# Products of zeros put in where TensorE's plan shows a wait, in the first units of a fused attention and token-mixing kernel

## The chip, the cores and the metric

The kernel runs on one core of one Trainium2 chip. The metric is device time in microseconds (us) of one execution; the number given for a kernel is the median of its runs. TensorE (PE in the profile) does the matrix products, VectorE (DVE), ScalarE (ACT) and GpSimd (POOL) the elementwise work, and SyncE's queue (SP) issues the transfers. Instructions of one engine run in the order in which they stand in the program.

## The reference

One block of a conditioned transformer, batch 1, 2048 tokens of width 512, all in bf16. The conditioning vector gives six vectors of width 512; then a windowed attention (32 heads of 16, each token sees itself and the 255 before it) and an MLP that mixes over tokens, each in a gated residual:

```python
mod = (_silu(c) @ w_mod).reshape(c.shape[0], 6, 1, -1)
sa, ca, ga, sb, cb, gb = (mod[:, n] for n in range(6))
h = _layernorm(x, axis=-1) * (1 + ca) + sa
x = x + ga * _A_ref(h, A_wqkv, A_wo)                   # sliding-window attention
h = _layernorm(x, axis=-1) * (1 + cb) + sb
x = x + gb * _B_ref(h, B_w1, B_b1, B_w2, B_b2)         # layernorm, then gelu(h over tokens @ w1 + b1) @ w2 + b2
```

## The kernel before

The 2048 tokens are 16 blocks of 128 and four groups of 512. The kernel has a hand-written start, a planned middle and a hand-written end.

**The start** (`warm`, `fm`, `turn`, lines 551 to 650) brings in the first tokens and weights, issues some 128x512 products of the tile `zero` with itself into a bank that nobody reads (`warm`, line 571; `WARM = (7, 1, 2)`), makes the modulation vectors, and turns, modulates and projects the first 256 tokens.

**The planned middle.** From there to about 165 us of the trace a planner decides, while the program is being built, in which order every engine's instructions stand. It keeps a clock of its own for each engine (`pe["t"]` for TensorE, `free[...]` for the others) in planned microseconds, asks for the earliest next step of each engine, emits the step that starts first, and moves that engine's clock on. TensorE's steps are of these kinds:

- a score step (`do_scores`, products on line 696): for a unit of a head group, the scores of four heads of 16, out of `QT` and `KT`, with the window's triangles added by products with `mask_w` and `mask_r`. It goes into one or two of three double banks of PSUM, named `t`. ACT takes the exponential of each (line 704, one `ACTIVATE` of 128x1024 or 128x768), and the bank is free after that;
- an attention step (`do_av`, line 721): exponentials times values for one head group, also into a `t` bank; DVE turns it (line 734) and divides;
- one product at a time of a dense group (`do_dense`) into one of two single banks named `dn`: the projections for queries and keys (line 356), which DVE or ACT copy out (lines 287, 369, 367), for values `V` (line 331, copied out on line 287), the turning of the normalized tokens of the first group (line 309, modulated on line 297), the broadcast modulation vectors (line 402), the output projection (line 432), and early parts of the MLP (line 470).

`pick_pe` picks between these; the main loop then calls the step with its planned start, `best[0]`. Where that is later than `pe["t"]`, TensorE waits by the plan. `issue` also books when TensorE's own instructions have to be fetched (`FIRST_BLOCK`, `BLOCK`, `FETCH`).

The tokens of the second group of 512 are normalized on DVE and POOL (`xn`, line 256), turned by four transfers of SP's queue (`turn_block`, line 305) into `h1T`, and modulated in place on DVE (line 297). SP's queue issues, in its fixed order: the weights, `wmod` (line 221), the biases, seven of the eight pieces of `wod` (line 224), the four turns, the last piece of `wod`, eight blocks of `x` (line 227), the broadcast vectors (line 418), the spread of keys `ks` into `KT` (line 385), the turns of the third group.

**The end** sums the first MLP product over all tokens (lines 462, 1334), applies gelu, and does the second product (line 1475) into the output.

A pool hands out a bank as a new tile each time; whoever writes the new tile first waits until the last use of the old one is over. If the old tile's last use was a write of TensorE itself that nobody read, the new writer waits for that write to be complete.

Of the kernel before, what the change touches and what calls it, by code (L numbers as in the profile page):

```python
# [8 lines left out]
DT = mybir.dt  # L9
# [3 lines left out]
P = 128  # L13
# [41 lines left out]
EARLY = 11  # L55
AHEAD = 14
PAUSE = 1.2
TURN_LAT = 2.5
FETCH, FIRST_BLOCK, BLOCK = 3.4, 193, 256
ODD = 0.31  # L60
# [3 lines left out]
def kernel(  # L64
# [14 lines left out]
    nc = tc.nc  # L79
# [62 lines left out]
    zero = modw.tile([P, 4 * P], DT.bfloat16, name="zero")  # L142
# [159 lines left out]
    def turn_block(tg, tl):  # L302
        if h1T[tg] is None:
            h1T[tg] = hpool.tile([P, ND, 4 * P], DT.bfloat16, name="h1T")
        dma.dma_start(out=h1T[tg][:, :, tl * P : (tl + 1) * P], in_=xn1[tg, tl][:], transpose=True)
# [219 lines left out]
    with tc.manual_schedule():  # L525

        dn_pools = [
            tc.alloc_tile_pool(name=f"ps_dn{n}", bufs=1, space=bass.MemoryType.PSUM, side="right") for n in range(2)
        ]
# [109 lines left out]
        t_pools = [tc.alloc_tile_pool(name=f"ps_t{n}", bufs=1, space=bass.MemoryType.PSUM) for n in range(3)]  # L639
# [154 lines left out]
        def publish(key, t):  # L794
            avail[key] = t
            for j in waiting.pop(key, []):
                j.settle()
# [96 lines left out]
        n = 2 * EARLY_HEADS  # L894
# [32 lines left out]
        def load_next(t):  # L927

            w1_state["busy"] = bool(loads)
            if not loads:  # L930
                return
            o, i = loads.pop(0)
            key = token()

            def then(t):
                loaded_at.append(t + 4.0)
                load_next(t + PAUSE)
            Job(lambda eng: eng.memset(o[:, 0:1], 0.0), {GE: 0.12}, gives=key, prio=4, at=t).settle()
            Job(lambda eng: dma.dma_start(out=o, in_=i), {YE: 0.6}, [key], prio=6, at=t, then=then).settle()
# [9 lines left out]
        def apply_jobs(tg, t, prio):  # L949
            used = [(k, tg - 2, g) for g in range(ND) for k in ("qd", "kd", "v") if tg > 1]  # L950
            for tl in range(4):
# [6 lines left out]
                    lambda eng, tl=tl: turn_block(tg, tl), {YE: 1.35}, [("x", tg, tl)] + used,  # L958
                    ("xt", tg, tl), 1, lat=TURN_LAT, at=t, then=lambda t, tl=tl: publish(("xe", tg, tl), t + 1.6),
                ).settle()  # L960
# [30 lines left out]
        pe = {"t": 0.0, "mode": "full", "group": (halves[2], 0), "s": 0, "av": 0, "n": 2 + 2 * (25 + 4 * ND + sum(WARM)), "block": -9.0}  # L991
        SWITCH = 0.094
        t_free, d_free = [0.0, 0.75, 0.0], [None, 0.0]
# [260 lines left out]
        def pick(e):  # L1254
            best = None
            able = [j for j in queue[e] if j.gate is None or j.gate()]
            if not able:
                return None
            first = min(begin(e, j) for j in able)
            if e == SE:  # L1260
                j = min((j for j in able if begin(e, j) <= first + 0.01), key=lambda j: (j.prio, j.seq))
            else:
                j = min((j for j in able if begin(e, j) <= first + VE_WIN), key=lambda j: (j.prio, j.seq))
            return begin(e, j), j

        def pick_pe():
            s, a, d, f = scores_start(), av_start(), dense_start(), first_start()
            if f and (a is None or f[0] < a[0] - 0.1) and (d is None or f[0] <= d[0] + 0.1):
                return f[0], do_first, f[1:]
            if a and (s is None or a[0] <= s[0] + AV_S) and (d is None or a[0] <= d[0] + AV_D):  # L1270
                return a[0], do_av, a[1:]
            if s and (d is None or s[0] <= d[0] + S_D):
                return s[0], do_scores, s[1:]
            if d:
                return d[0], do_dense, d[1:]
            return None

        while True:
            best = pick_pe()
            for e in (SE, VE, GE, YE):  # L1280
                c = pick(e)
                if c and (best is None or c[0] < best[0]):
                    best = c[0], e, c[1]
            if best is None:
                break
            if callable(best[1]):
                best[1](best[0], *best[2])
                continue
            start, e, j = best
            queue[e].remove(j)  # L1290
            j.emit(ENG[e])
            free[e] = start + j.opts[e]
            if e == VE and j.opts[e] == FAST:
                fast_until[0] = free[e]
            if j.then:
                j.then(free[e])
            if j.gives:
                publish(j.gives, free[e] + j.lat)
# [150 lines left out]
    with tc.tile_pool(name="ftmp", bufs=3) as ftmp, tc.tile_pool(  # L1449
        name="ps_y0", bufs=4, space=bass.MemoryType.PSUM  # L1450
    ) as ps_y0, tc.tile_pool(name="ps_y1", bufs=4, space=bass.MemoryType.PSUM) as ps_y1:
        for tg in range(NT // 4):
# [20 lines left out]
            for fc, (tl, lo, hi) in order:  # L1473
# [3 lines left out]
                    rhs=gated[fc][:] if last and (lo, hi) == LAST[-1] else guT[fc][:, lo:hi],  # L1477
                    start=(fc == 0), stop=(fc == NF - 1),
# [51 lines left out]
```

## Time and profile before

| what | us |
|---|---|
| median of 3 runs | 247.29 |
| the runs | 247.29, 250.26, 246.52 |
| the profiled execution, device time | 248.87 |
| its span, from the first to the last instruction | 246.7 |
| outside the span (248.87 - 246.7) | 2.17 |
| busy in the span: PE, DVE, ACT | 229.8, 190.0, 158.5 |

Times within the trace are counted from the start of the span. A row of the timeline gives the start, the length, the engine, the line, the operation with its tiles, shapes and the number of merged instructions; in square brackets stands the idle time of the engine before the row and what ended it, where there was a notable wait. In a row of stretches, `PEclk` is the share of its full clock that TensorE was granted.

### The profile page before, as it was taken

The page shows a single profiled execution, that of the slowest core. Times are in us where ns is not written, and L with a number is a line of the kernel's source. Part 1 is how long each engine was busy: PE and PEld are TensorE (multiplying, and loading weights), DVE is VectorE, ACT ScalarE, POOL GpSimd, SP SyncE. Part 2 cuts the span into 40 slices and gives each one's busy share as a digit, 9 for nine tenths or more (in the row PEclk, how much of TensorE's full clock was granted, in tenths as well). Part 3 has the DMA queues.
Part 4 walks back from the last instruction along what each step waited for, and adds up shares of the span by engine and source line. Part 5 has one row for each costly group of instructions (what it writes and reads, how often), then busy time and mean ns, then how long its engine had stood idle before and what let it go on. Part 6 is the DMA issues. An engine that isn't in the chain of part 4 may idle for free.

```text
span 246.7 us, 8687 instructions
## 1 busy us (share of the span) xinstructions
PE 229.8 (93%) x3691; PEld 122.6 (50%) x3723; DVE 190.0 (77%) x416; ACT 158.5 (64%) x182; POOL 69.7 (28%) x158
## 2 busy tenths in 40 slices
PE   5877999999999788999999999999999999999995
PEld 2544675655566365454454554544444444444444
DVE  5697679998999999999997989957974632543564
ACT  3495897999999898999999999950108700000000
POOL 7636104332272332423413624403540000000000
PEclk9996899999999999999999999999999999999999
DMA  6994455287573611010013131059995000201031
GB/s 202 314 351 129 88 148 131 43 139 160 168 98 74 152 25 27 5 21 3 9 23 79 51 88 45 3 169 352 415 409 224 0 3 0 85 23 64 27 103 43
DMA packets 32042, 27.70 MB, mean 112 GB/s; under 512 B 16516, under 2 KB 27652, under 8 KB 32004
## 3 DMA queue, kind: packets, MB, share of 16 engines
q1 hardware_dynamic: 31708, 26.63, 38.3%
q8 instruction: 29, 0.48, 0.9%
q10 hardware_dynamic: 296, 0.53, 0.6%
q14 instruction: 9, 0.07, 0.1%
HBM read 22.03 MB, written 2.10 MB: 98 GB/s over the span
## 4 chain that ended last, share of the span: by engine, by line
PE 74%; DVE 12%; ACT 6%; DMA 3%; issue 3%; SPq 0%; DVEq 0%; ACTq 0%
PE py L1475 20%; PE t L696 12%; PE dn L470 9%; PE dn L356 7%; PE t L462 6%; ACT et L704 6%; PE t L721 5%; PE dn L331 4%; PE dn L432 4%; PE t L1334 3%; DVE KT L369 3%; DMA wmod<-in_w_mod_dram 2%; PE pu L1334 2%; DVE QT L287 1%; PE pa L1370 1%
## 5 line engine op out<-in xcount | busy, mean ns | idle before, releaser
L704 ACT ACTIVATE et<-t 128x1024 bf16<-128x1024 f32 (+1 forms) x142 | 131.8, 1021 | 8.0 <-PE t L696 7.3
L1475 PE MATMUL py<-guT,w2r 128*128 128x512 bf16 (+2 forms) x234 | 47.7, 363 | 0.2
L696 PE MATMUL t<-QT,KT 32*128 32x64 bf16 (+4 forms) x752 | 38.0, 253 | 1.4 <-ACT et L704 0.9
L356 PE MATMUL dn<-h1T,wqkv 128*128 128x512 bf16 (+1 forms) x140 | 33.6, 357 | 4.9 <-DVE QT L287 1.8
L1475 PEld LDWEIGHTS <-w2r 128*128 128x128 bf16 x252 | 23.5, 98 | 25.4 <-DVE gelu_a L1357 0.4
L748 POOL TENSOR_TENSOR merge<-t,zr 128x512 bf16<-128x512 f32 (+1 forms) x16 | 21.5, 1346 | 42.8 <-DVE zr L743 42.7
L1490 DVE SCALAR_TENSOR_TENSOR o<-py,bFM,bc_gb 128x512 bf16<-128x512 f32 (+2 forms) x17 | 12.1, 711 | 24.5 <-PE py L1475 23.0
L696 PEld LDWEIGHTS <-KT 32*128 32x128 bf16 x752 | 13.9, 93 | 27.0 <-issue 25.1
L696 PE MATMUL t<-mask_r,mask_w 32*128 32x128 bf16 (+3 forms) x432 | 24.8, 223 | 0.4 <-issue 0.4
L470 PE MATMUL dn<-hb,w1hi 128*128 128x512 bf16 x91 | 23.9, 381 | 0.9 <-issue 0.6
L734 DVE STREAM_TRANSPOSE t<-t 128x1024 f32<-128x1024 f32 x16 | 19.8, 1236 | 4.2 <-PE t L721 4.1
L356 PEld LDWEIGHTS <-wqkv 128*128 128x128 bf16 x160 | 14.2, 102 | 16.3 <-issue 4.5
L231 POOL TENSOR_SCALAR ln_ve<-ln_mv 128x1 f32<-128x1 f32 x32 | 7.7, 241 | 48.0 <-DVE ln_mv L831 39.4
L235 POOL TENSOR_TENSOR ln_rstd<-ln_ve,mhalf 128x1 f32<-128x1 f32 x32 | 19.2, 601 | 2.7
L721 PEld LDWEIGHTS <-V 64*32 64x32 bf16 x1504 | 16.5, 91 | 6.6 <-issue 6.3
L721 PE MATMUL t<-et,V 64*32 64x320 bf16 (+4 forms) x1384 | 19.3, 251 | 0.0
L331 PE MATMUL dn<-wqkv,h1T 128*64 128x256 bf16 x256 | 17.6, 276 | 1.4 <-DVE V L287 0.9
L696 PEld LDWEIGHTS <-mask_w 32*128 32x128 bf16 x432 | 14.1, 95 | 2.7 <-issue 0.6
L331 PEld LDWEIGHTS <-h1T 128*64 128x64 bf16 x256 | 12.9, 109 | 3.4 <-issue 2.4
L470 PEld LDWEIGHTS <-w1hi 128*128 128x128 bf16 x98 | 8.1, 97 | 10.5 <-issue 3.0
L432 PE MATMUL dn<-wod,OTd 128*128 128x512 bf16 x43 | 12.2, 381 | 0.7 <-issue 0.3
L287 DVE CAST V<-dn 128x512 bf16<-128x512 f32 x15 | 10.1, 676 | 2.1 <-PE dn L331 2.1
(123 smaller groups left out, 289.3 us busy)
## 6 DMA issues: line engine op xcount, KB each, us to landing
w2r<-in_B_w_dram SPq DMA_DIRECT2D x14, 512.0 KB, 10.2
w1hi<-in_B_w_dram SPq DMA_DIRECT2D x11, 320.0 KB, 4.0
w1b<-in_B_w_dram SPq DMA_DIRECT2D x5, 448.0 KB, 6.7
x<-in_A_x_dram SPq DMA_DIRECT2D x16, 128.0 KB, 3.6
wmod<-in_w_mod_dram SPq DMA_DIRECT2D x4, 512.0 KB, 9.3
out_dram<-otile SPq DMA_DIRECT2D x15, 128.0 KB, 1.7
wqkv<-in_B_w_dram SPq DMA_DIRECT2D x11, 128.0 KB, 2.8
wqkv<-in_A_wqkv_dram SPq DMA_DIRECT2D x4, 256.0 KB, 6.0
```

The source lines that it names most:

```text
L235: nc.gpsimd.tensor_tensor(out=r[:], in0=ve[:], in1=mhalf[:, 0:n], op=ALU.pow)
L331: nc.tensor.matmul(pv[CH * par : CH * par + CH, 256 * ch : 256 * ch + 256].rearrange("p (h d) -> p h d", d=DH), lhsT=h1T[tg][:, dc, t0 : t ...
L356: nc.tensor.matmul(pq[:, 0:n_cols], lhsT=wqkv[:, dc, col0 : col0 + P], rhs=h1T[tg][:, dc, cols], start=(dc == 0), stop=(dc == ND - 1),)
L432: nc.tensor.matmul(pa[:], lhsT=tokens_of(OTd[tg][g], tl), rhs=wod[:, g, :], start=(g == 0), stop=(g == ND - 1),)
L462: nc.tensor.matmul(first[k][1][:, n, :], lhsT=w1_of(sc, 2 * k + n), rhs=hb[sc][:], start=(sc == 0), stop=(sc == NT - 1),)
L470: nc.tensor.matmul(ps[:], lhsT=w1_of(s0 + n, fc), rhs=hb[s0 + n][:], start=(n == 0), stop=(s0 + n + 1 == s1),)
L696: nc.tensor.matmul(o, lhsT=w, rhs=r, start=start, stop=stop, tile_position=(row, 0), skip_group_check=True,)
L704: nc.scalar.activation(out=state["e", u][:, 2 * a : 2 * a + 2, 0:w], in_=ps[:, :, 0:w], func=ACT.Exp, scale=SCORE_SCALE,)
L721: nc.tensor.matmul(chunks(o, qs), lhsT=Vring[kc // GC % 3][rows, kc % GC, h : h + 32], rhs=e[:, at : at + len(qs), :], start=first, stop=F ...
L734: nc.vector.transpose(out=v["t"][:].rearrange("p a c -> p (a c)"), in_=po[:].rearrange("p a c -> p (a c)"))
L748: eng.tensor_tensor(out=v["m"][:].rearrange("p (b d h) -> p h b d", d=DH, h=4)[:, :, lo:hi], in0=view()[:, :, lo:hi, 0:DH], in1=v["z"][:, ...
L1475: nc.tensor.matmul(pys[tl, lo, hi][:, 0 : hi - lo], lhsT=w2r[:, fc, tb * P : (tb + 1) * P], rhs=gated[fc][:] if last and (lo, hi) == LAST[ ...
```

## The change

A function `keep_busy` is called before each step of TensorE with the planned start of that step. If the plan shows a wait of at least 0.35 planned us that ends before `BUSY_UNTIL` (24 planned us), and one of the three `t` banks or two `dn` banks is free by the plan within 0.1 us, it takes a tile of the first such pool and issues one product of `zero` with itself, 128x512, for each 0.25 us of the wait less 0.1. Nobody reads the result. The planner's clock and its count of TensorE's instructions stay as they were, so all later decisions are the same.

```diff
@@ -55,6 +55,7 @@
 PAUSE = 1.2
+BUSY_UNTIL = 24.0
 TURN_LAT = 2.5
@@ -1275,6 +1276,17 @@
+        def keep_busy(until):
+
+            n = int((until - pe["t"] - 0.1) / 0.25)
+            pools = [
+                pool for pool, x in [*zip(t_pools, t_free), *zip(dn_pools, d_free)] if x is not None and x < pe["t"] + 0.1
+            ]
+            if n > 0 and pools and until < BUSY_UNTIL and pe["t"] > 0:
+                ps = pools[0].tile([P, 4 * P], DT.float32, name="dn" if pools[0] in dn_pools else f"t{t_pools.index(pools[0])}")
+                for _ in range(n):
+                    nc.tensor.matmul(ps[:], lhsT=zero[:, 0:P], rhs=zero[:], start=True, stop=True)
+
         while True:
             best = pick_pe()
@@ -1284,6 +1296,7 @@
             if callable(best[1]):
+                keep_busy(best[0])
                 best[1](best[0], *best[2])
                 continue
```

In the program this adds nine products with nine weight loads, at seven places on TensorE (7466 rows instead of 7448), all into `t` banks. Nothing moves on DVE, ACT, POOL or SP. Counted in order, places 1 to 4 get one product each, place 5 two, place 6 one, place 7 two:

1. before the eight projections that follow the first scores;
2. before the second score step;
3. before the third score step;
4. before the fourth score step;
5. before the last two key and query projections ahead of the fifth score step;
6. among the projections after the next score steps, where a `dn` bank is waited for;
7. before the score step that follows the turning of the biases (line 422).

Place 2 on TensorE, before. `t0`, `t1` and `t2` are the three banks for scores, a new number is a new tile:

```order
L356 MATMUL dn_437<-h1T_310,wqkv_132 128x256
L696 LDWEIGHTS KT0_167
L696 MATMUL t1_449<-QT1_421,KT0_167 128x256
L696 LDWEIGHTS KT0_167
L696 MATMUL t0_450<-QT1_421,KT0_167 128x256 [waits Activation_49]
```

The same place now (all line numbers are 1 or more higher, since the change adds lines):

```order
L357 MATMUL dn_439<-h1T_310,wqkv_132 128x256
L1288 LDWEIGHTS zero_134
L1288 MATMUL t1_451<-zero_134 128x512 [waits PE_49]
L697 LDWEIGHTS KT0_167
L697 MATMUL t1_453<-QT1_421,KT0_167 128x256 [waits PE_49]
L697 LDWEIGHTS KT0_167
L697 MATMUL t0_454<-QT1_421,KT0_167 128x256 [waits Activation_49]
```

The product of zeros takes the bank `t1` that the scores are about to take, and the first score product now waits until it is complete (`waits PE_49`); the wait of the second bank for ACT stands where it stood. At places 3, 4 and 7 the first score product waits for the product of zeros in the same way, and the wait for ACT has moved from it to the product of zeros.

Place 5 on TensorE, before:

```order
L356 MATMUL dn_565<-h1T_310,wqkv_132 128x256
L356 LDWEIGHTS wqkv_132 [waits DVE_49]
L356 MATMUL dn_578<-h1T_310,wqkv_132 128x256 [waits PE_49]
L356 MATMUL dn_578<-h1T_310,wqkv_132 128x256
L696 LDWEIGHTS KT0_167 [waits DVE_49]
L696 MATMUL t1_583<-QT0_374,KT0_167 128x64 [waits Activation_49]
L696 MATMUL t0_584<-QT0_374,KT0_167 128x64 [waits Activation_49]
```

The same place now:

```order
L357 MATMUL dn_573<-h1T_310,wqkv_132 128x256
L1288 LDWEIGHTS zero_134
L1288 MATMUL t0_586<-zero_134 128x512 [waits Activation_49]
L1288 MATMUL t0_586<-zero_134 128x512
L357 LDWEIGHTS wqkv_132 [waits DVE_49]
L357 MATMUL dn_589<-h1T_310,wqkv_132 128x256 [waits PE_49]
L697 MATMUL t1_594<-QT0_374,KT0_167 128x64 [waits DVE_49]
L697 MATMUL t0_595<-QT0_374,KT0_167 128x64 [waits PE_49]
```

Two products of zeros stand ahead of the projection that waits for DVE, in the bank `t0`; they wait for ACT to have left that bank, and the score product that uses it next waits for them, a few products later.

## The prediction
> **What bounds the kernel now.** I read the page first: its span, and the line of TensorE's granted clock by fortieths (6.17 us each).
>
> ```profile
> span 246.7 us, 8687 instructions
> PE 229.8 (93%) x3691; PEld 122.6 (50%) x3723; DVE 190.0 (77%) x416; ACT 158.5 (64%) x182; POOL 69.7 (28%) x158
> PEclk9996899999999999999999999999999999999999
> ```
>
> PE is busy 93% of the span, so whatever delays PE early is hard to win back. Its clock is full except in the fourth and fifth slices. The second view cuts that place into stretches of 3.41 us, half of the slow time, with two later stretches for comparison:
>
> ```profile
> core 0: us, PE busy (x) PEld busy (x) DVE busy (x) ACT busy (x) POOL busy (x), PEclk, DMA share, GB/s
> 13.43:16.84 3.41, 2.80 (x48) 1.87 (x48) 3.38 (x9) 3.41 (x5) 1.13 (x5) 1.00 1.11 350
> 16.84:20.26 3.42, 1.75 (x32) 0.96 (x26) 3.38 (x11) 2.50 (x3) 1.06 (x3) 1.00 1.07 320
> 20.26:23.67 3.41, 2.90 (x34) 1.79 (x34) 2.21 (x7) 2.68 (x3) 3.17 (x2) 0.50 0.27 64
> 23.67:27.09 3.42, 3.42 (x35) 1.88 (x37) 2.54 (x8) 1.90 (x3) 0.96 (x2) 0.50 0.26 65
> 81.69:85.10 3.41, 2.17 (x20) 0.96 (x20) 3.38 (x6) 3.41 (x5) 1.98 (x4) 1.00 0.60 121
> 242.10:245.51 3.41, 1.60 (x29) 1.42 (x26) 1.64 (x5) 0.00 (x0) 0.00 (x0) 1.00 0.27 77
> ```
>
> The clock is exactly half from 20.26 to 27.09, 6.83 us. Right before, PE was busy 1.75 of 3.42 us, with DVE as the bound (3.38 of 3.42). Busy time alone does not decide: 1.60 us at the end of the program was not punished. But those are products on the whole array, and in 16.84 to 20.26 a good part is score products on 32 rows. With 2.17 us the clock held. After the drop, 2.90 busy us did not bring it back, 3.42 did.
>
> Third, PE's timeline around the seven places:
>
> ```profile
> 2.63 3.17 PE L571 MATMUL h<-zero 128*128 128x512 bf16 x7
> ...
> 11.36 0.25 PE L696 MATMUL t<-mask_r,mask_w 32*128 32x192 bf16 x4
> 11.71 1.13 PE L356 MATMUL dn<-h1T,wqkv 128*128 128x256 bf16 x8
> 12.77 0.53 PE L696 MATMUL t<-QT,KT 32*128 32x256 bf16 x10
> ...
> 13.50 1.05 PE L356 MATMUL dn<-h1T,wqkv 128*128 128x256 bf16 x8
> 14.48 0.65 PE L696 MATMUL t<-QT,KT 32*128 32x256 bf16 x10
> ...
> 15.80 0.79 PE L309 MATMUL dn<-identity,xn 128*128 128x128 bf16 x8 [0.51 <-DVE QT L287]
> 16.52 0.43 PE L696 MATMUL t<-QT,KT 32*128 32x256 bf16 x10
> ...
> 17.95 1.05 PE L356 MATMUL dn<-h1T,wqkv 128*128 128x256 bf16 x8 [0.82 <-DVE h1T L297]
> 19.84 0.39 PE L356 MATMUL dn<-h1T,wqkv 128*128 128x256 bf16 x2 [0.85 <-DVE KT L369]
> ...
> 23.39 1.23 PE L356 MATMUL dn<-h1T,wqkv 128*128 128x256 bf16 x5 [0.52 <-DVE QT L287]
> ...
> 25.20 1.89 PE L356 MATMUL dn<-h1T,wqkv 128*128 128x256 bf16 x8
> ...
> 28.40 0.39 PE L696 MATMUL t<-QT,KT 32*128 32x256 bf16 x8 [0.27 <-ACT et L704]
> ```
>
> Eight projections take 1.05 us at full clock and 1.89 at half. The places begin at 11.71, 12.77, 14.48, 16.52, 19.84, 23.39 and 28.40: at the first four the trace has no wait, at the last three it has 0.85, 0.52 and 0.27 us. Two real waits (15.80 and 17.95) get nothing. The first row also shows that products of zeros count as work for the clock: the start has little else, and the clock comes up behind it.
>
> **The cost of the nine products.** At full clock 49 products of 128x512 in a row take 10.74 us, 0.219 each, and one from start to completion is 0.379; at half clock the seven of the start give 3.17 / 7 = 0.453 each.
>
> ```profile
> 198.35 10.74 PE py L1475 x49
> L1475 PE MATMUL py<-guT,w2r 128*128 128x512 bf16 x184 | 40.4, 379 | 0.2
> 11.89 7.45 ACT L704 ACTIVATE part<-t 128x1024 bf16<-128x1024 f32 x8
> 20.99 1.94 ACT L704 ACTIVATE part<-t 128x1024 bf16<-128x1024 f32 x2 [1.65 <-PE t L696]
> ```
>
> Place 1: 0.22. At places 2, 3 and 4 the next score product takes the same bank and waits for completion: 0.38 each. Together 0.22 + 3 x 0.38 = 1.36 us on PE, in a stretch where DVE is busy 3.38 of each 3.4 us and PE then waits 0.51 + 0.82 + 0.85 = 2.18 us for DVE. So they eat waits. The first to suffer is the fifth exponential: eight in a row take 0.93 each, so it starts at 11.89 + 4 x 0.93 = 15.6, and its scores, done by about 15.2 (14.48 + 0.65), come 0.22 + 2 x 0.38 = 0.98 later, so it is some 0.6 us late; but ACT idles 1.65 us behind its eighth (11.89 + 7.45 to 20.99), which covers it. On the path: 0, at worst 0.5, if DVE finds one input late. Place 5: 0.44 in a wait of 0.85: 0. Place 6: 0.22 (at half clock 0.45) in 0.52: 0. Place 7: 0.22 + 0.38 = 0.60 against 0.27, so up to 0.33 as the trace stands; at full clock PE comes there sooner and the wait for ACT is longer, so 0. All these covers are DVE's and ACT's work; without them the nine cost 5 x 0.22 + 4 x 0.38 = 2.6 us.
>
> The 18 new rows also shift where PE's code is fetched. The trace has no row for this; the nearest is a wait with no other releaser:
>
> ```profile
> 39.33 0.40 PE L696 MATMUL t<-QT,KT 32*128 32x64 bf16 x12 [0.22 <-issue]
> ```
>
> I take 0, with both ends at two such waits: 0.4 less (two go) to 0.4 more (two come in addition).
>
> **What the clock gives.** In the stretch that dropped it, place 5 adds 0.44 us of products on the whole array, and place 4, near its edge, up to 0.22: 1.75 + 0.44 = 2.19 to 2.41 us, above the 2.17 that held. So I expect the clock to hold. Then PE's 2.90 + 3.42 = 6.32 us of slow work would take half: at most 3.16 less. But DVE has 2.21 + 2.54 = 4.75 us of its own work there, more than ACT's 4.58, so the 6.83 us cannot shrink below 4.75: 2.08 us less at 28.40. I take 2.1.
>
> What is late next? The values and the first attention step:
>
> ```profile
> 32.17 0.69 DVE L287 CAST V<-dn 128x512 bf16<-128x512 f32 x1 [0.18 <-PE dn L331]
> 32.78 0.40 DVE L297 TENSOR_SCALAR h1T<-h1T,modFM 128x512 bf16<-128x512 bf16 x1
> 33.61 0.69 DVE L287 CAST V<-dn 128x512 bf16<-128x512 f32 x1 [0.43 <-PE dn L331]
> 34.22 1.05 DVE L297 TENSOR_SCALAR h1T<-h1T,modFM 128x512 bf16<-128x512 bf16 x3
> 34.48 0.71 PE L721 MATMUL t<-part,V 64*32 64x256 bf16 x46
> 24.50 0.59 SPq L224 DMA_DIRECT2D wod<-in_A_wo_dram  x1
> 25.21 6.06 SPq L305 DMA_TRANSPOSE h1T<-xn  x4
> 31.96 5.02 SPq L227 DMA_DIRECT2D x<-in_A_x_dram  x8
> 37.66 0.78 SPq L418 DMA_DIRECT2D bc_ga<-bc_rows  x1
> L305 SPq DMA_TRANSPOSE h1T<-xn x4: 1200/1216/2142, 25.2 to 30.1; - x4
> DMA to landing us min/median/max: 2.4/2.4/3.4
> SPq L224 <- DMA wmod<-in_w_mod_dram: 4.4, 3, 2.2
> ```
>
> SP's queue issues the `wod` pieces, which had waited 4.4 us for `wmod` to land, and then the four turns without a break: the last starts at 30.1 and lands 2.4 later, at 32.5. None of that hangs on PE's clock. DVE's modulation of `h1T` at 32.78 stands ahead of the fourth copy of `V`, and that copy ahead of the attention step. With PE 2.1 us sooner, DVE stands at `h1T` until 32.5; the modulation takes 0.35 (1.05 / 3), the copy 0.69: 33.54. The attention step, which began at 34.48 because PE came no sooner, begins at about 33.6: 0.9 us is left of the 2.1. Behind it SP's queue is again in the way: the eight blocks of `x` end at 36.98, so the broadcast vectors issued at 37.66, and behind them the keys and the turns of the third group, come at most 0.68 us earlier. I take 0.6.
>
> The sum: span 246.7 - 0.6 = 246.1, device time 248.87 - 0.6 = 248.3 where the profiled execution had 248.87. That one lies 1.58 above the median of 247.29; carrying the difference over, 247.29 - 0.6 = **246.7 us**. About 2% (4.9 us) is what a measurement of this kernel can tell from no change.
>
> **Rivals.**
>
> A, the whole gain arrives. The four turns have inputs from DVE and POOL; if the first of them wait for those and not for the queue, they move up with PE. Their unbroken issue (6.06 us, minimum 1.2 each) speaks against it, the 2.14 of the first for it. Then 2.1 us remain: 245.2.
>
> B, nothing to win in the timed runs. The six slow microseconds are known from one execution, the slower of four but one; where the stretch falls differently, other executions may never have been slow, and the median stays: 247.3, with place 7 up to 247.6.
>
> C, the clock falls for another reason. The longest wait of PE before the drop is 0.85 us, yet the clock fell. [...] In rows: the clock stays at half from 20.26 to 27.09, place 6 costs 0.45 in 0.52, and place 7, still at full clock behind 27.09, 0.33: 247.6.
>
> D, slower than before. The products stand on PE's path where the plan is wrong about the waits, and the clock falls nevertheless: nine at 0.453 and four completions at twice 0.16 (0.379 - 0.219) are 4.1 + 1.3 = 5.4 us, 252.7. It decides once the chain of waits runs through line 1288 instead of DVE's lines between 11 and 20 us. DVE's 3.38 of 3.41 and 3.42 us speak against it.
>
> **How the numbers follow.** Forecast 0.63, A 0.13, B 0.12, C 0.07, D 0.05. The likeliest gives 246.7. The low end takes A with the code fetch's 0.4 at its best, 244.8; the high end takes C and B with 0.4 for the fetch, 0.5 for a late input at places 1 to 4, and another 0.6 because the known executions reach from 246.52 to 250.26: 249.1. D lies outside. Faster by over 2% would be below 242.3, which even the 3.16 us of the clock with the 0.4 (243.7) does not reach: 0.03 for what I don't see. Slower by over 2%, above 252.2, is D: 0.05. Within: 0.92.
>
> **What would show it.** Right, if the clock line has no dip in its fourth and fifth slices; if eight projections near 25 us take 1.05 instead of 1.89; if PE reaches the score step of 28.40 about 2 us earlier; if a wait of about 1 us appears ahead of the attention step's first product, put down to DVE's `V`, with the four turns still at 25.2 to 31.3; and if `bc_ga` is issued near 37.0. The turns moving up shows A. A dip that stays shows C; an unchanged median beside a trace without the dip shows B. Idle ACT or DVE between 12 and 20 us, released by PE, shows D's products on the path. The prediction would be wrong above all if the first group's stretch is not bound by DVE once PE is 1.4 us later, or if SP's queue lets more through than 0.6.

## The result, and the profile after

| | kernel before | changed kernel |
|---|---|---|
| median, us | 248.09 (20 runs, 246.52 to 253.21) | 249.08 (20 runs, 246.59 to 251.43) |
| ratio | | 1.0052, 95% interval 1.0026 to 1.0077 |
| profiled execution: device time, span, us | 248.87, 246.7 | 247.73, 245.6 |

Ratios, and the means by clock further below, leave out executions over 1.5% above the fastest of the same kernel.

The changed kernel is slower by half a per cent, clear of noise though far under 2%. A repetition gave 1.0087 (1.0053 to 1.0120). The forecast was 246.7, a little faster. The profiled execution looks like the forecast: its span is 1.1 us shorter. It was a lucky one of the 20, and what seems to have made the others slower is in it too.

The page of the changed kernel, its span, clock and the shares of the chain of work that ended last (no piece of that chain lies on line 1288, which was rival D's sign):

```profile
span 245.6 us, 8703 instructions
PEclk9999999999999999999999999999999999999999
PE 71%; DMA 11%; DVE 9%; ACT 4%; issue 3%; SPq 1%; DVEq 0%; ACTq 0%
```

The same stretches as in the prediction, in the changed kernel (length, busy time of PE, PEld, DVE, ACT, POOL with instructions, granted clock, DMA share, GB/s):

```profile
16.84:20.26 3.42, 2.18 (x37) 1.52 (x38) 3.39 (x10) 2.05 (x4) 1.58 (x3) 1.00 1.05 304
20.26:23.67 3.41, 2.71 (x37) 1.58 (x31) 3.30 (x10) 3.41 (x4) 3.28 (x4) 1.00 0.21 52
23.67:27.09 3.42, 3.05 (x56) 2.11 (x59) 2.65 (x8) 3.15 (x5) 0.33 (x1) 1.00 0.52 110
```

PE is busy 2.18 us where it was 1.75, DVE 3.39 where it was 3.38, and the clock stays full. Now PE's timeline of the changed kernel, from its first score step on:

```profile
10.62 0.40 PE L697 MATMUL t<-QT,KT 32*128 32x256 bf16 x12
...
20.37 0.83 PE L357 MATMUL dn<-h1T,wqkv 128*128 128x256 bf16 x6
...
26.12 0.40 PE L697 MATMUL t<-QT,KT 32*128 32x64 bf16 x10 [0.27 <-PE dn L423]
...
33.53 0.26 PE L722 MATMUL t<-et,V 64*32 64x128 bf16 x9 [0.24 <-issue]
...
34.64 0.41 PE L722 MATMUL t<-part,V 64*32 64x256 bf16 x24
...
35.69 0.35 PE L697 MATMUL t<-QT,KT 32*128 32x192 bf16 x12
35.86 0.24 PE L697 MATMUL t<-mask_r,mask_w 32*128 32x128 bf16 x5
37.54 0.20 PE L697 MATMUL t<-mask_r,mask_w 32*128 32x64 bf16 x3 [1.43 <-issue]
37.68 1.25 PE L357 MATMUL dn<-h1T,wqkv 128*128 128x512 bf16 x4
...
40.90 0.41 PE L722 MATMUL t<-part,V 64*32 64x256 bf16 x24
```

And the same places of the kernel before:

```profile
11.13 0.40 PE L696 MATMUL t<-QT,KT 32*128 32x256 bf16 x12
...
36.45 0.41 PE L721 MATMUL t<-part,V 64*32 64x256 bf16 x24
...
37.67 0.25 PE L696 MATMUL t<-mask_r,mask_w 32*128 32x128 bf16 x8
37.85 1.25 PE L356 MATMUL dn<-h1T,wqkv 128*128 128x512 bf16 x4
39.33 0.40 PE L696 MATMUL t<-QT,KT 32*128 32x64 bf16 x12 [0.22 <-issue]
...
41.23 0.41 PE L721 MATMUL t<-part,V 64*32 64x256 bf16 x24
```

The score step of 28.40 comes at 26.12, 2.3 us sooner, and the second attention step at 34.64 instead of 36.45, 1.8 us sooner. The third comes at 40.90 instead of 41.23: only 0.3 us is left. Not all of this is the change's doing: the first score step, ahead of all seven places, already comes at 10.62 instead of 11.13, and of the 1.1 us by which the span is shorter, 0.8 come behind the third attention step. Between the second and the third attention step stands the new wait of 1.43 us, with no releaser that the profile shows, three products before the end of a score step. Before, the nearest such wait was 0.22 us, and it stood behind the next four projections.

What such a wait goes with, the transfers show. The DMA view of the changed kernel from 34 to 37.5 us, its line of the queue for instructions:

```profile
q8 instruction: 1, 0.02, 2.7%
```

And the same line of the page, for the whole span (packets, MB, share of 16 engines):

```profile
q8 instruction: 29, 0.48, 0.8%
```

The queue named for instructions moved 29 pieces in the program, 0.48 MB / 29 = 16.6 KB each, and 7466 rows / 29 = 257 rows each if all of them hold PE's; one of them falls into the stretch of the wait. By the records of its packets it landed at 36.31, and PE went on at 37.54, 1.23 us later. In the kernel before a piece landed at 38.04, and the wait of 0.22 us ended at 39.33, 1.29 later. So it is in every profiled execution below that waits at this place: PE goes on 1.2 to 1.6 us after a piece has landed, while the pieces around it start 3.5 to 5.5 us apart. That the awaited piece is PE's code is an inference from this, from the count, and from how the wait moves with the number of rows, below.

### The profile page after: what moved, and what is told of

Read it like the earlier page. It is cut to its first block, busy times and chain, and to the rows that moved or that the text cites. A ratio compares the mean times of both kernels' runs of the same rounds, so it can differ in the third digit from the quotient of the medians.

```text
span 245.6 us, 8703 instructions
## 1 busy us (share of the span) xinstructions
PE 228.6 (93%) x3698; PEld 122.6 (50%) x3732; DVE 189.7 (77%) x416; ACT 158.5 (65%) x182; POOL 69.5 (28%) x158
## 4 chain that ended last, share of the span: by engine, by line
PE 71%; DMA 11%; DVE 9%; ACT 4%; issue 3%; SPq 1%; DVEq 0%; ACTq 0%
PE py L1488 20%; PE t L697 11%; PE dn L471 9%; PE t L463 6%; DMA wmod<-in_w_mod_dram 5%; PE t L722 5%; PE dn L357 5%; ACT et L705 4%; PE dn L332 4%; PE dn L433 4%; PE t L1347 3%; DMA wqkv<-in_A_wqkv_dram 3%; PE pu L1347 2%; DMA h1T<-xn 2%; PE pa L1383 1%
## 5 line engine op out<-in xcount | busy, mean ns | idle before, releaser
L697 PE MATMUL t<-QT,KT 32*128 32x64 bf16 (+4 forms) x752 | 36.7, 250 | 1.3 <-ACT et L705 0.7
L357 PE MATMUL dn<-h1T,wqkv 128*128 128x512 bf16 (+1 forms) x140 | 31.6, 338 | 4.6 <-DVE QT L288 1.8
L697 PE MATMUL t<-mask_r,mask_w 32*128 32x128 bf16 (+3 forms) x432 | 24.2, 220 | 1.4 <-issue 1.4
L357 PEld LDWEIGHTS <-wqkv 128*128 128x128 bf16 x160 | 13.6, 97 | 14.9 <-issue 4.9
L722 PEld LDWEIGHTS <-V 64*32 64x32 bf16 x1504 | 16.6, 90 | 7.1 <-issue 6.7
```

The costliest lines, as they stand in the source:

```text
L357: nc.tensor.matmul(pq[:, 0:n_cols], lhsT=wqkv[:, dc, col0 : col0 + P], rhs=h1T[tg][:, dc, cols], start=(dc == 0), stop=(dc == ND - 1),)
L697: nc.tensor.matmul(o, lhsT=w, rhs=r, start=start, stop=stop, tile_position=(row, 0), skip_group_check=True,)
L722: nc.tensor.matmul(chunks(o, qs), lhsT=Vring[kc // GC % 3][rows, kc % GC, h : h + 32], rhs=e[:, at : at + len(qs), :], start=first, stop=F ...
```

## The experiments

Rows count PE's instructions against the kernel before. Each kernel ran beside the kernel before, on the same chip.

### The kernel before again, and rows without work

The first ran the kernel before unchanged:

> The kernel before, unchanged, to learn the granted clock and the span of each of its executions; of the kernel before only one clock was known (0.986). Theory 1 (the dip is a matter of each execution, and the products of zeros cure it, but code fetching takes the gain back): ratio 1.000 within 0.3%, and at least half of the executions with a clock near 0.986, against 4 of 20 for the changed kernel. Theory 2 (most executions of the kernel before never dip, so there was nothing to win): ratio the same, but most clocks at 0.998 to 1.000.

Ratio 1.0012 (0.9979 to 1.0045). Of its 12 executions, 4 had a clock of 0.986, 6 about 0.992, 2 were at full clock: the dip is a matter of each execution, as theory 1 says, but neither count that was expected came. 0.986 is two slow stretches of 3.4 us (at half clock from 20.26 to 27.09, 6.83 us in a span of 246.7, the first profile gives 1 - 6.83 / 2 / 246.7 = 0.986), 0.993 by the same sum is one. More such counts are in the table below.

The second put the 18 rows into the start:

```diff
+        def tiny(n):
+            for _ in range(n):
+                nc.tensor.matmul(warm_ps[:, 0:1], lhsT=zero[:, 0:P], rhs=zero[:, 0:1], start=True, stop=True)
         warm(WARM[1])
+        tiny(9)
```

> Nine products of zeros of one column each, ahead of the wait for wmod in the start: the same 18 rows more on PE, so the same shift of the places at which PE's code is fetched, but no work for the clock and no bank waits among the first units. Theory 1a (the shift by 18 rows is what costs): 1 to 1.5 us slower than before, ratio 1.004 to 1.006, and a wait without a releaser of over 1 us near 36 us as in the changed kernel. Theory 1b (fetching is late because PE comes sooner at full clock, whatever the shift): no slower than before, ratio 0.998 to 1.002, with the dip as often as before. Theory 3 (the products or their bank waits cost): ratio 1.000.

Ratio 1.0038 (1.0004 to 1.0072), and its timeline:

```profile
37.49 0.20 PE L701 MATMUL t<-mask_r,mask_w 32*128 32x64 bf16 x3 [1.43 <-issue]
37.63 1.25 PE L356 MATMUL dn<-h1T,wqkv 128*128 128x512 bf16 x4
```

The same wait of 1.43 us at the same three products from the end, without any product of zeros among the units. Nine rows of weights and nine products of next to no work suffice for it. Theory 1b is not out by this run alone, since this execution has no dip near 20 us and PE came sooner here too; the versions with no row more, below, tell the two apart.

### Fewer products, and the planner told

Place 5 alone (`8 < pe["t"] < 9` in the condition), 4 rows:

> Only the two products of place 5, so 4 rows more instead of 18 and no bank wait at places 2, 3, 4, 7. If the shift costs (1a): the clock mostly holds and the time is up to 1 us under the kernel before, ratio 0.995 to 0.999. If fetching is late at full clock whatever the shift (1b): clock held, ratio 0.999 to 1.003, the wait without a releaser stays between 33 and 40 us. If the products and bank waits of the other places cost (3): faster than the changed kernel by over 0.3%, with the same wait without a releaser.

Ratio 1.0012 (0.9978 to 1.0047), one of 12 executions at 0.986. The expected gain did not come, and the interval allows it. The profiled execution has its two slow stretches at 8.49 and 18.73 us, both ahead of the products of place 5, which stand at 20.43. It has waits of 0.49 in the first attention step and of 0.83 behind two of the four projections:

```profile
38.15 0.82 PE L357 MATMUL dn<-h1T,wqkv 128*128 128x512 bf16 x2
39.80 0.59 PE L357 MATMUL dn<-h1T,wqkv 128*128 128x512 bf16 x2 [0.83 <-issue]
```

Then all nine, with the rows added to the planner's count:

```diff
             if n > 0 and pools and until < BUSY_UNTIL and pe["t"] > 0:
+                pe["n"] += 2.01 * n
```

> All nine products, and the planner told of their rows (it adds them to its count of PE's instructions), so that it plans around the fetches where they now fall; the order changes from the first broadcast products on. If the shift costs (1a): below the changed kernel by about 1 us, ratio to the kernel before 0.996 to 1.001. If fetching is late because the planner's times for it are too short (1b): like the changed kernel, 1.003 to 1.007, with waits without a releaser of over 1 us between 30 and 45 us.

Ratio 1.0338 (1.0282 to 1.0394). Its waits without a releaser between 30 and 45 us are 0.59 and 0.16, against 1.43 in the changed kernel, so the new order avoids most of that wait; but everything behind it stands in another order, and some 8 us are lost elsewhere; where is open. It says nothing on the 18 rows.

### Rows in steps, and products without rows

Eight rows in the start (`tiny(4)`), a single execution:

> Four one-column products in the start instead of nine: 8 rows more on PE. Theory 1a (the shift costs, because the code fetch that fell behind four 128x512 projections, where PE needed few rows in 0.86 us, falls ahead of them): the wait without a releaser near 36 to 39 us is 0.2 + 4 x 0.22 = 1.1 us if the shift reaches just past the four projections, 0.2 to 0.3 us shorter than the 1.43 of 18 rows; with 4 rows it was 0.83. Theory 1b (the size of the shift does not matter): 1.4 or 0.2, like one of the two known, not between.

```profile
37.95 0.39 PE L356 MATMUL dn<-h1T,wqkv 128*128 128x512 bf16 x1
39.55 0.81 PE L356 MATMUL dn<-h1T,wqkv 128*128 128x512 bf16 x3 [1.20 <-issue]
```

The wait is 1.20 us, between 0.83 at 4 rows and 1.43 at 18, and stands behind one projection instead of two.

Products at places 3, 4 and 5, one each, for which the start's three later ones go (`4 < pe["t"] < 9`, one product per place, `WARM = (7, 0, 0)`): no row more.

> One full product of zeros at each of places 3, 4 and 5, and the three products of zeros that stood between the start's own products left out: no row more from there on, so code is fetched where it was before. Theory 1a: no wait over 0.6 us without a releaser between 33 and 40 us, few executions with a clock of 0.986, and the time at or up to 0.3% below the kernel before (0.997 to 1.000). Theory 3 (the products and bank waits cost on PE's path): 1.002 or more, although the rows are the same in number.

Ratio 0.9999 (0.9970 to 1.0027); none of 12 executions at 0.986; no wait without a releaser between 33 and 40 us in the profiled one. It has a wait of 0.79 us behind the four projections, which the profile puts down to DVE's copy `ks`; but in the kernel before, the same product went on at 39.33 while that copy ran until 39.62, so it doesn't wait for `ks`, and PE went on 1.46 us after a piece of the instruction queue had landed. By the ratio the products and their bank waits cost nothing that can be seen.

All nine at their places, one column wide (`ps[:, 0:1]`, `rhs=zero[:, 0:1]`):

> All nine products at their seven places, in the same banks with the same waits, but one column wide: the same rows and waits, almost no work for the clock. Theory 1a: 1.43 us without a releaser near 36 us, a ratio of 1.004 to 1.008, and the dips of the kernel before (half of the executions). Theory 3: ratio near that of the nine one-column products in the start (1.0038) plus what the bank waits cost, 0.1 to 0.3%.

Ratio 1.0067 (1.0023 to 1.0110); 3 of 8 executions without a dip. The wait expected near 36 us is only 0.22 in the profiled execution, because another stands ahead of it. DVE's and PE's timeline:

```profile
29.64 0.69 DVE L288 CAST V<-dn 128x512 bf16<-128x512 f32 x1 [0.25 <-PE dn L332]
...
32.87 0.41 DVE L298 TENSOR_SCALAR h1T<-h1T,modFM 128x512 bf16<-128x512 bf16 x1 [2.54 <-DMA h1T<-xn]
33.19 0.68 DVE L288 CAST V<-dn 128x512 bf16<-128x512 f32 x1
...
34.02 1.05 PE L722 MATMUL t<-part,V 64*32 64x256 bf16 x48 [2.01 <-DVE V L288]
```

This is the wait that the prediction worked out: DVE stands 2.54 us at `h1T` until the turns have landed, the fourth copy of `V` queues behind it, and the attention step waits 2.01 us. Behind it the wait near 36 us is 0.22, against 1.43 in the changed kernel: most of it seems hidden here. One of 1.07 us, without a releaser, ends at 119.35.

Places 4 and 5, one product each, and two of the start's left out (`WARM = (7, 1, 0)`), again no row more:

> As the one before last, with one product at each of places 4 and 5 and only two of the start's products left out. Theory 1a: 0.997 to 1.001, no wait over 0.6 us without a releaser between 33 and 40 us, some executions with a clock of 0.986 left. Theory 3: 1.001 or more, in proportion to two products.

Ratio 0.9991 (0.9963 to 1.0020), no execution of 12 at 0.986. As in the version before the last, the wait behind the four projections, here 0.54 us, is put down to DVE.

### The changed kernel again, and a version with two rows less

> The changed kernel again, beside the next one and with the clock of every execution of both kernels known. Theory 1a: slower than before by 0.3 to 0.8%, and slower also when only executions of both kernels without a dip are compared (by about 1 us), so that the loss is not the clock's. If the clock makes the loss (theory 4: the new wait makes new dips), executions without a dip are level within 0.3 us and those with one are more frequent than before.

Ratio 1.0087 (1.0053 to 1.0120), a little more than the 0.8% that was expected at most. The wait is 1.70 us in the profiled execution. This one had two dips, one from 8.78 to 12.19 and one here (stretches as above):

```profile
36.09:39.50 3.41, 1.65 (x47) 0.78 (x25) 1.57 (x3) 0.97 (x2) 1.33 (x1) 1.00 0.59 136
39.50:42.91 3.41, 3.41 (x32) 1.40 (x31) 2.48 (x6) 2.87 (x4) 1.34 (x1) 0.50 0.18 38
```

Around the wait PE had only 1.65 us of work in 3.41, and the clock fell behind it, to 0.50 from 39.50 on: in this execution a dip stands where the kernel before has none in its profile. That the wait made it is not shown. But 9 of 12 executions had no dip and were still slow, at 249.31 us in the mean, so the dip is the smaller part.

The version with places 4 and 5 and `WARM = (7, 0, 0)`, 2 rows less than before:

> One product at each of places 4 and 5, and all three of the start's later products left out: 2 rows less than before, so the code fetch falls one projection later. Theory 1a: the wait without a releaser near 38 to 40 us is at most 0.2 us, the ratio 0.996 to 1.000, and under the changed kernel of the same call by 0.4 to 0.9%. Theory 3: between the two, over 1.001.

Ratio 0.9979 (0.9946 to 1.0012), beside 1.0087 for the changed kernel. The wait was 0.69 in the profiled execution, longer than expected, and one product further on, behind all four projections.

> The last version again, to narrow its interval: 0.9979 in the first five rounds. Theory 1a: 0.996 to 1.000, and no clock below 0.99. If the first result was chance: above 1.001, or as many executions at 0.986 as in the kernel before.

Again 0.9974 (0.9947 to 1.0002), no execution of 24 at 0.986, and no wait of 0.2 us there.

### The control for the rows

The start's three later products left out and nothing put in, 6 rows less:

> The kernel before without the three later products of zeros of the start, and nothing put in: 6 rows less. It tells the code fetch from the clock in the last kernel. If the gain there is the rows' alone: the wait without a releaser near 38 to 40 us at most as long as with 2 rows less (0.69 at full clock), ratio 0.996 to 0.999, as with the products at places 4 and 5. If the products at places 4 and 5 are worth something by the clock: ratio 0.998 to 1.003, with dips of two windows (clock near 0.986) in 15 to 25% of the executions, against none in 36 executions of the three kernels with two or three products.

Ratio 0.9933 (0.9897 to 0.9969), with a wait of 0.23 us three products behind the four projections:

```profile
37.37 0.20 PE L696 MATMUL t<-QT,KT 32*128 32x64 bf16 x3
37.81 0.38 PE L696 MATMUL t<-QT,KT 32*128 32x64 bf16 x9 [0.23 <-issue]
```

It was run again beside two others: three one-column products in place of the three left out (rows as before), and the changed kernel without those three (12 rows more).

> The kernel with 6 rows less again: 0.9933 (0.9897 to 0.9969) before. If that was no chance: 0.990 to 0.997, with dips in half of the executions, among them some at 0.986.

> The start's three later products of zeros left out and three one-column products put in their stead: as many rows as before, almost no work. If the rows decide (1a): 0.998 to 1.002, that is 0.5% above the kernel with 6 rows less. If the left-out products themselves were what cost (theory 5): 0.990 to 0.997, like the kernel with 6 rows less.

> The changed kernel without the start's three later products: 12 rows more than before instead of 18. If the rows decide (1a): the wait without a releaser still over 1.2 us, ratio 1.003 to 1.009, as the changed kernel, since past four projections more rows cost little more. If theory 5: 0.6% below the changed kernel, 0.998 to 1.003.

Measured: 1.0001 (0.9959 to 1.0043), 1.0012 (0.9975 to 1.0048) and 1.0073 (1.0040 to 1.0107). So much of the 0.9933 was chance: the expectation of 0.990 to 0.997 is missed, and the two together lie near 0.997. The rows put back without the products give no loss, and 12 rows give the changed kernel's loss, with the wait in full (this profile puts it down to a DMA, at the same place):

```profile
36.46 0.25 PE L697 MATMUL t<-mask_r,mask_w 32*128 32x128 bf16 x8
38.29 1.24 PE L357 MATMUL dn<-h1T,wqkv 128*128 128x512 bf16 x4 [1.58 <-DMA x<-in_A_x_dram]
```

### Together

The wait at this place, by rows, with where it stands as seen from the four projections between the two score steps:

| rows | products of zeros among the units | where the wait stands | length, us | ratio |
|---|---|---|---|---|
| -6 | none | 3 score products behind them | 0.23, 0.25 | 0.9933, 1.0001 |
| -2 | places 4, 5 | 1 score product behind them | 0.69, none | 0.9979, 0.9974 |
| 0 | none (before) | behind all four | 0.22, 0.27 | 1, 1.0012 |
| 0 | none (one-column products in the start) | put down to DVE | 0.55 | 1.0012 |
| 0 | 3 to 5; 4, 5 | put down to DVE | 0.79, 0.54 | 0.9999, 0.9991 |
| +4 | place 5 | behind two | 0.83 | 1.0012 |
| +8 | none | behind one | 1.20 | not measured |
| +12 | all nine | ahead of all four | 1.58 | 1.0073 |
| +18 | none | 3 score products ahead of them | 1.43 | 1.0038 |
| +18 | all nine | 3 score products ahead of them | 1.43, 1.70 | 1.0052, 1.0087 |
| +18 | all nine, one column wide | ahead of all four, behind a wait of 2.01 for DVE | 0.22 | 1.0067 |

More rows move the wait towards the start of the program, by about one product for two rows (less between 4 and 12), and from behind the four projections to ahead of them it grows from 0.22 to 1.58 us, 1.36 us for projections that take 1.25. That looks like a fetch of code after a fixed number of rows, though no trace says what a piece holds: once the four projections, 1.25 us of work with few rows, no longer lie in front of it, nothing hides it.

Theory 1b has a share. In the three versions with no row more where the wait is put down to DVE, the four projections begin at 36.86, 35.86 and 37.12 instead of 37.85, and the wait is 0.55, 0.79 and 0.54 instead of 0.22: coming sooner lengthens it too, by 0.3 to 0.6 us. But their ratios are at 1, and those with 12 or 18 rows more at 1.0038 to 1.0087. It is not shown that the wait near 37 us is the whole loss of the latter. Of the four profiled executions with 18 rows in the planned order, three have another between 118 and 120 us that ends 1.3 to 1.5 us after a piece has landed (0.84, 1.07 and 0.60 us, the first and the last put down to ACT); neither of the kernel before has one there.

The executions by clock, of all runs whose clocks are known (the mean time in us of those compared, and how many these are of how many):

| | no dip (0.997 and up) | one stretch (near 0.993) | two (near 0.986) | all |
|---|---|---|---|---|
| kernel before | 247.48 (56 of 56) | 247.82 (51 of 54) | 249.12 (16 of 27) | 247.84 (123 of 137) |
| changed kernel | 248.85 (24 of 25) | 249.33 (2 of 2) | 250.17 (3 of 5) | 249.02 (29 of 32) |
| two or three products, 0 or -2 rows | 247.58 (33 of 33) | 247.18 (15 of 15) | none | 247.45 (48 of 48) |

The listed clock says less than it seems to. It counts the time before the trace's first record of the clock as full. In the control with three one-column products, listed at 1.000, the last five projections of the start take 1.27 us; in the kernel before, listed at 0.986, the same five take 0.71:

```profile
8.50:12.00 3.50, 3.30 (x16) 2.09 (x15) 1.94 (x5) 1.49 (x4) 2.01 (x7) 1.00 1.15 320
11.13 1.27 PE L356 MATMUL dn<-h1T,wqkv 128*128 128x256 bf16 x5
10.43 0.71 PE L356 MATMUL dn<-h1T,wqkv 128*128 128x256 bf16 x5
```

(The first two rows are the control's, the third the kernel before's.) Of the six profiled executions without a dip, the first record of a full clock stands between 11.39 and 13.79 us in five, and at 6.26 in the changed kernel's. Of the eight with slow stretches of 3.4 us that do not follow each other, six have one that begins between 8.49 and 9.25 us, ahead of all seven places, where nothing of the change can reach it. So "no dip" and "one stretch" can hold executions with much the same clock, and the means of these two columns do not price a slow stretch: those with one are 0.34 us slower than those with none in the kernel before, and 0.40 us faster in the small versions.

## Why the prediction was wrong

**The step that failed** is the price of the code fetch: "I take 0, with both ends at two such waits: 0.4 less (two go) to 0.4 more (two come in addition)". The mechanism was named (that the wait is for code is inferred, no run shows it), its size was not: the trace shows one wait growing from 0.22 to 1.43 us and one of 0.24 ahead of it, and by executions without a dip the changed kernel is 248.85 - 247.48 = 1.37 us slower. The bound was drawn from waits as they stood and not from what stood in front of them: the wait of 0.22 us at 39.33 was the rest of a longer one, with 1.25 us of projections, in the row just above it, as its cover. A shift by 18 rows could take that cover away, and a bound of 0.22 + 1.25 = 1.47 us could have been read from those two rows.

**What the clock is worth** was taken off the wrong execution, for a reason that rival B names. The median execution of the kernel before is not one with two slow stretches: only 27 of 137 are, 54 have one, 56 none. Mean less no dip is 247.84 - 247.48 = 0.36 us by the executions compared, and 0.60 by all 137; that the second is the forecast's 0.6 is luck, since those with two stretches are 1.64 us slower than those with none, and few. How much of the 1.64 is the clock's is not shown. The changed kernel keeps 0.17 of dips (249.02 - 248.85). By this reckoning, which the mixed columns above make a rough one, the dips gave back 0.19 and 1.37 us are lost without them: 1.18 us slower, against 0.52% or 1.3 us measured.

**The clock held** from 20 to 27 us in the profiled execution, as forecast. Over all executions this is shown for the small versions: none of 48 has two slow stretches, against 27 of 137 of the kernel before. Of the 48, 36 have the start without its three later products; the two versions with that start (one with three one-column products in their place) and nothing among the units have two slow stretches in 5 of 34 executions. For the changed kernel it is not shown: 5 of 32 still have two, and in the one that was profiled they lie near 9 us and behind the new wait. Rival C did not hold: by these counts the dips of two stretches go in the small versions, which have products of zeros among the units. The longest wait between 8 us and the dip at 20.26 is 0.85 us; what length of wait would lower the clock is not shown. The forecast's own measure, PE's busy time against the 2.17 us that held, was no measure: the clock fell behind 2.51 and 2.81 busy us and held behind 1.94 (last section). DVE hid places 1 to 4 as forecast (the fifth score step comes at 19.71 instead of 20.17, so the lead of 0.5 us that the first one had is kept), and place 7 cost nothing that shows (0.27 us of wait remain there, where a second product of zeros stands that the trace has no record of).

**The next wait** was right as a mechanism, and not always the one that decides. In the profiled execution of the changed kernel the turns were issued at 23.55 instead of 25.21, since the loads ahead of them landed sooner there (the sixth piece of `wod`, which waits for `wmod` to land, went out at 22.21 instead of 23.88), `bc_ga` at 35.85 instead of near 37.0, and the attention step did not wait; in the run with one-column products it waited 2.01 us for just this. Where it does not, the gain of about 2 us runs on into the wait near 37 us, some four microseconds later. In the changed kernel's execution 0.3 us of it passes 41 us, less than the 0.5 by which it was ahead before the first place.

**The range** held the median, 249.08 in 244.8 to 249.1, by a hair, and by luck: its upper end was added up from rivals B and C, a late input and the scatter, with 0.4 for the fetch that took more. The sign was wrong.

**What stays open:** where the changed kernel's remaining dips lie in most of its executions (one trace shows one behind the new wait and one near 9 us); how the loss of some 1.3 us divides between the wait near 37 us and those behind it; what makes the loads land up to 2 us sooner in some executions; and whether the version with 2 rows less beats the kernel before, at 0.9979 and 0.9974 with intervals that both reach 1.

## What to carry to other kernels

Instructions that do no work can still cost time: here 18 rows of next to no work in the start moved a wait without a releaser from behind four projections to ahead of them, and it grew from 0.22 to 1.43 us. Where a profile shows a short wait without a releaser, look at what stands just ahead of it and price the wait without that cover. Pay for added instructions with others taken away ahead of the dense part: two products of zeros with two fewer in the start left no execution of 12 with two slow stretches, at no loss (0.9991). And take a gain that depends on the clock from the clocks of many executions, not from the one that was profiled.

## What the runs showed of the hardware that was not expected

The granted clock fell to 0.50 behind 1.75 busy us of PE in 3.42 with a longest wait of 0.85 (16.84 to 20.26 in the kernel before), and behind 1.65 of 3.41 with one of 1.70 us (36.09 to 39.50 in the changed kernel's second profile). It stayed there 6.83 us in the first case and 3.41 in the second. PE's busy time does not decide it. Of the stretches below, the clock fell behind the first two (place 5 alone; the changed kernel again) and not behind the third (nine one-column products):

```profile
15.32:18.73 3.41, 2.51 (x44) 1.29 (x41) 3.38 (x11) 3.41 (x5) 0.04 (x1) 1.00 1.10 348
5.37:8.78 3.41, 2.81 (x44) 1.73 (x44) 2.38 (x7) 0.69 (x2) 2.45 (x10) 1.00 1.06 333
16.84:20.26 3.42, 1.94 (x36) 1.51 (x37) 3.38 (x10) 2.05 (x4) 1.52 (x3) 1.00 1.07 298
```

What does decide it is not shown. That products of zeros count as work for it fits the start of the kernel before, where the first record of a full clock stands at 6.61 us behind seven of them at 0.453 us each and little else, and it fits none of 36 executions with two slow stretches against 5 of 34 without such products among the units. It is not shown beyond that: of the changed kernel, with nine such products, 5 of 32 have two.

Executions with two slow stretches of the kernel before are 1.64 us slower than those with none, less than half of the 6.8 us at half clock; what of the rest is covered by other work was not measured.
